# Attention and mixer on one core: q and k of batches 1 to 3 turned by DMA, scores in 64 rows, PSUM banks 4/2/2

## The chip, the cores and the metric

The kernel runs on one core of a Trainium2 chip. The metric is the device time of an execution in microseconds (us). A profiled execution also gives a trace; its span runs from the first to the last instruction. Engine names in profiles: PE is TensorE's matmul, PEld its weight load, DVE is VectorE, ACT is ScalarE, POOL is GpSimd, SP is SyncE; L376 is line 376 of the kernel that was profiled.

## The reference

Four batches of eight heads, 768 positions, head size 64. First a windowed attention with a distance bias, then a mixer with a low-rank product over the positions and a feed-forward of width 2048:

```python
scores = scale * np.matmul(q, k.transpose(0, 1, 3, 2))
rel = pos[:, None] - pos[None, :]
is_global = pos[None, :] < 8
is_local = (rel >= 0) & (rel < 96)
dist = np.where(is_global & ~is_local, 96.0, np.abs(rel))
scores = np.where(is_global | is_local, scores - slopes[:, None, None] * dist, -1e9)
a = softmax(scores)                      # over the last axis
x = np.matmul(a, v)                      # then heads side by side: (B, 768, 512)
h = x.transpose(0, 2, 1) @ U @ V         # U (768, 32), V (32, 768)
u = x + h.transpose(0, 2, 1)
out = u + np.maximum(u @ w_ch1, 0.0) @ w_ch2
```

## The kernel before

A *pair* is two heads of one batch, so there are 16 pairs, four to a batch; pair i belongs to batch i // 4. The 768 positions are six blocks of 128. Because the window is shorter than a block, a block of keys meets only its own block of queries and the next, where the eight global keys ride in eight places of the neighbour block (kA, vA).

For each pair these steps run:

- `load_qk`: two DMAs on SP's queue bring q and k of two heads as fp32 (tiles qst, kst, three buffers each; runs of 1536 bytes, position p * 6 + n in partition p). `cast_qk` makes fp16 (q16, k16, two buffers), on POOL except at the very start. `load_v`: two DMAs on POOL's queue, one per head, which convert to fp16 on the way, in runs of 64 elements (four buffers).
- `st_T`: six PE transposes each for q and k, into two PSUM tiles `tp`; ScalarE and VectorE copy them out as z[0], z[1] (tile qz, one per head, with zeros in the other head's 64 rows) and kT; kA is copied from kT with the global keys put in.
- Scores (`scores`): per head eleven 128x128 matmuls that contract over 128 rows, of which the other head's 64 are zero in qz; three chunks c of at most 512 columns, each in one PSUM tile `sc`. Batch 0 (`st_SE`) adds the bias by one more matmul and takes the exponential out of PSUM. Batches 1 to 3 (`st_S`) add the bias on VectorE with a scalar_tensor_tensor into sp (fp32, one buffer per head), and `st_E` takes the exponential of a whole head on ScalarE (tile ep).
- `st_V`: eleven matmuls per head into `ob`, normalised by VectorE into x_sb, then copied by POOL to fp16 as x16.
- `st_M1` and `st_M2`: the low-rank product (PSUM tiles tmp_ps and ups), written as uT by VectorE and ScalarE.

When a batch's attention is done, `queue_ff` puts its feed-forward into the deque `units`: per half batch 16 up units (`mk_up`: four matmuls into PSUM tile hps, then a Relu on ScalarE into htr) and twelve down units (`mk_down`: a quarter of a 128-row output tile each, in PSUM tile cps). `fill(n)` emits n of them between the attention steps of the next batch, 14 per pair. Batch 3's feed-forward runs alone at the end.

PSUM has eight banks, divided by tag: `sc` has three, `oc` two (ob and cps), `th` three (tp, tmp_ps, ups, hps).

Batch 0 is emitted under `manual_schedule`, that is, in the written order. After `ordered.close()` the tile framework's scheduler decides the order of each engine's queue; every queue then executes in order, so an instruction that waits holds up all that stand behind it on its engine. DMAs issued by POOL stand in POOL's queue among its copies and also wait for the eighth DMA before them on that queue.

Of the kernel before, what the change touches and what calls it, by code (L numbers as in the profile page):

```python
# [11 lines left out]
FP32 = mybir.dt.float32  # L12
FP16 = mybir.dt.float16
# [3 lines left out]
ALU = mybir.AluOpType  # L17
# [3 lines left out]
def kernel(  # L21
# [13 lines left out]
    nc = tc.nc  # L35
    B, H, S, D = q.shape
    NG = int(n_global)
    NL = int(n_local)
    P = 128
    DM = H * D  # L40
    NSB = S // P
# [4 lines left out]
    NP = H // 2  # L46
    qk_scale = 1.0 / math.sqrt(D)
# [5 lines left out]
    slope = [2.0 ** (-8.0 * (h + 1) / H) for h in range(H)]  # L53
# [5 lines left out]
    W = 256 * NSB - P  # L59
# [5 lines left out]
    stp = ctx.enter_context(tc.tile_pool(name="stp", bufs=2))  # L65
    kp = ctx.enter_context(tc.tile_pool(name="kp", bufs=2))
    scp = ctx.enter_context(tc.tile_pool(name="scp", bufs=2))
# [3 lines left out]
    psum = ctx.enter_context(tc.tile_pool(name="psum", bufs=1, space=bass.MemoryType.PSUM))  # L71

    def ps_sc():
        return psum.tile([P, 512], FP32, name="sc", tag="sc", bufs=3)

    def ps_oc(name):
        return psum.tile([P, 512], FP32, name=name, tag="oc", bufs=2)

    def ps_th(name, dtype=FP32, cols=512):
        return psum.tile([P, cols], dtype, name=name, tag="th", bufs=3)  # L80


    NVB = 4
# [2 lines left out]
    def load_qk(i):  # L86
        b, h0 = i // NP, 2 * (i % NP)
        got = []
        for src, nm in ((q, "qst"), (k, "kst")):
            st = stp.tile([P, 2, NSB, D], FP32, name=nm, tag=nm, bufs=3)  # L90
            nc.sync.dma_start(
                st.rearrange("p h n d -> p h (n d)"),
                src[b, h0:h0 + 2].rearrange("h (p n) d -> p h (n d)", n=NSB),
            )
            got.append(st)
        staged[i] = got

    def cast_qk(i, eng):
        got = []
        for st, nm in zip(staged.pop(i), ("q16", "k16")):  # L100
            st16 = stp.tile([P, NSB, 2, D], FP16, name=nm, tag=nm, bufs=2)
            eng.tensor_copy(st16.rearrange("p n h d -> p h n d"), st)  # L102
            got.append(st16)
        cast[i] = got

    def load_v(i):
        b, h0 = i // NP, 2 * (i % NP)
        vt = vbuf[i % NVB]
        for hi in range(2):
            nc.gpsimd.dma_start(  # L110
                vt[:, hi, :, 0:D], v[b, h0 + hi].rearrange("(n p) d -> p n d", p=P)
            )
        vts[i] = vt

    NPAIR = B * NP
    staged, cast, vts = {}, {}, {}


    ordered = ExitStack()
# [9 lines left out]
    def warm(n):  # L129
# [12 lines left out]
        out=relB, in_=relB, compare_op=ALU.is_ge, fill=BIG,  # L142
# [3 lines left out]
        out=relB, in_=relB, compare_op=ALU.is_ge, fill=BIG,  # L146
# [13 lines left out]
    def slopes(h0, h1):  # L160
        for h in range(h0, h1):
            nc.vector.tensor_scalar_mul(slI[:, h], ident16, slope[h] / qk_scale)
# [8 lines left out]
    relcat = cst.tile([P, 3, 256], FP32, name="relcat")  # L171
# [39 lines left out]
    kts, kas, vas = {}, {}, {}  # L211

    def st_T(i):
        stq, stk = cast.pop(i)
        kT = kp.tile([P, S], FP16, name="kT", tag="kT")
        kA = kp.tile([P, NSB - 1, P], FP16, name="kA", tag="kA")
        tps = []
        for st in (stq, stk):

            tp = ps_th("tp", FP16, S)  # L220
            tps.append(tp.rearrange("d (n p) -> d p n", n=NSB))
            for n in range(NSB):
                nc.tensor.matmul(  # L223
                    tp[:, n * P:(n + 1) * P], st[:, n].rearrange("s h d -> s (h d)"), ident16,
                    is_transpose=True, start=(n == 0), stop=(n == NSB - 1),
                )
        tq, tk = tps
        z = qz[i % 2]
        nc.scalar.copy(z[0][0:D].rearrange("d (p n) -> d p n", n=NSB), tq[0:D])
        nc.vector.tensor_copy(kT.rearrange("d (p n) -> d p n", n=NSB), tk)  # L230
        nc.vector.tensor_copy(kA.rearrange("d n p -> d (n p)"), kT[:, 0:S - P])  # L231
        nc.vector.tensor_copy(
            kA[:, 1:, 0:NG], kT[:, 0:NG].unsqueeze(1).broadcast_to((P, NSB - 2, NG))
        )
        nc.vector.tensor_copy(z[1][D:P].rearrange("d (p n) -> d p n", n=NSB), tq[D:P])  # L235
        kts[i], kas[i] = kT, kA

    def st_A(i):
        vt = vts[i]
        vA = vap.tile([P, 2, NSB - 1, D + 1], FP16, name="vA", tag="vA")  # L240
        nc.gpsimd.tensor_copy(vA, vt[:, :, 0:NSB - 1])  # L241
        nc.vector.tensor_copy(
            vA[0:NG, :, 1:],
            vt[0:NG, :, 0:1].broadcast_to((NG, 2, NSB - 2, D + 1)),
        )
        vas[i] = vA

    sps, eps = {}, {}

    def scores(i, hi, c, on_pe):  # L250
        h = 2 * (i % NP) + hi
        kT, kA, z = kts[i], kas[i], qz[i % 2][hi]
        sc = ps_sc()
        c0 = 512 * c
        tot = min(512, W - c0)
        r0 = 256 if c else 0
        if on_pe:
            nc.tensor.matmul(
                sc[:, 0:tot], slI[:, h], rel16.rearrange("p a c -> p (a c)")[:, r0:r0 + tot], start=True, stop=False
            )  # L260
        for kb in (2 * c, 2 * c + 1):
            o = 256 * kb - c0
            nc.tensor.matmul(  # L263
                sc[:, o:o + P], kT[:, kb * P:(kb + 1) * P], z[:, kb * P:(kb + 1) * P],
                start=(o == 0 and not on_pe), stop=(o + P == tot),
            )
            if kb < NSB - 1:
                nc.tensor.matmul(  # L268
                    sc[:, o + P:o + 2 * P], kA[:, kb], z[:, (kb + 1) * P:(kb + 2) * P],
                    start=False, stop=(o + 2 * P == tot),  # L270
                )
        return sc, c0, tot, r0

    def st_SE(i, c):

        if c == 0:
            for hi in range(2):
                eps[i, hi] = scp.tile([P, W], FP16, name=f"ep{hi}", tag=f"ep{hi}")
        for hi in range(2):
            sc, c0, tot, _ = scores(i, hi, c, True)  # L280
            nc.scalar.activation(  # L281
                eps[i, hi][:, c0:c0 + tot], sc[:, 0:tot], AF.Exp, scale=qk_scale
            )

    def st_S(i, c):
        if c == 0:
            sps[i] = [
                scp.tile([P, W], FP32, name=f"sp{hi}", tag=f"sp{hi}", bufs=1)
                for hi in range(2)
            ]  # L290
        relf = relcat.rearrange("p a c -> p (a c)")
        for hi in range(2):
            sc, c0, tot, r0 = scores(i, hi, c, False)
            nc.vector.scalar_tensor_tensor(  # L294
                out=sps[i][hi][:, c0:c0 + tot], in0=sc[:, 0:tot],
                scalar=qk_scale / slope[2 * (i % NP) + hi], in1=relf[:, r0:r0 + tot],
                op0=ALU.mult, op1=ALU.add,
            )
# [129 lines left out]
    for i in range(NP):  # L428
        st_SE(i, 0)
        if i == 0:  # L430
            cast_qk(2, nc.gpsimd)
        if i >= 2:
            st_M1(i - 2)
        else:
            warm(1)
        if i:
            st_V(i - 1, 0)
            st_V(i - 1, 1)
        if i == 0:
            load_v(3)  # L440
        if i:
            cast_qk(i + 2, nc.gpsimd)
        st_SE(i, 1)
        st_T(i + 1)
        if i < 3:
            slopes(2 * i + 2, 2 * i + 4)
        if i:
            load_qk(i + 3)
        if i >= 2:
            st_M2(i - 2)  # L450
        if i == 1:
            for c in range(4):
                load_w1(c)
        st_SE(i, 2)
        st_A(i)
        if i >= 2:
            load_v(i + 2)
        if i == 2:
            table(relcat)
        if i == 3:  # L460
            for c in range(4):
                load_w2(c)
# [10 lines left out]
    new_batch(1)  # L473
    for i in range(NP, NPAIR):
        b, hp = divmod(i, NP)
        if i + 3 < NPAIR:
            load_qk(i + 3)
        if i + 2 < NPAIR:
            load_v(i + 2)
        st_A(i)  # L480
        for c in range(3):
            st_S(i, c)
            fill(1)
        st_E(i, 0)
        st_E(i, 1)
        if i > NP:
            st_M2(i - 1)
            if hp == 0:
                queue_ff(b - 1, 0)
                queue_ff(b - 1, 1)  # L490
        fill(2)
        if i + 1 < NPAIR:
            if hp == NP - 1:
                new_batch(b + 1)
            st_T(i + 1)
        if i + 2 < NPAIR:
            cast_qk(i + 2, nc.gpsimd)
        fill(3)
        st_V(i, 0)
        fill(2)  # L500
        st_V(i, 1)
        fill(3)
        st_M1(i)
        fill(1)
# [39 lines left out]
```

## Time and profile before

| | |
|---|---|
| runs of the kernel (us) | 281.81, 284.34, 282.52; median 282.52 |
| span of the profiled execution | 279.8 us (its own device time is not listed; the runs lie 2.0 to 4.5 above this span) |
| PE busy | 255.3 us, 91% |
| PEld busy | 156.1 us, 56% |
| DVE, ACT, POOL busy | 147.8, 123.2, 87.2 us |
| mean granted TensorE clock | 0.963 |
| DMA packets | 42327, 26.64 MB; 26912 under 512 bytes |

Busy times overlap and matmuls are pipelined: a 128x128 matmul counts 0.22 us from its start to its end, while the next one may start 0.055 us after it. In what follows the start-to-start time is used for TensorE's work. In the group lines the columns are: line, engine, operation, output<-input by tile names, shape, count, busy us and mean ns of one, and the idle time of that engine just before the group with what ended it. In the lines in order of time the columns are start, duration (to the end of the last one where several are merged), engine, line, operation; in square brackets stands the idle time before. In the table of DMA issues the last column is the median time from issue to landing in us.

### The profile page before, as it was taken

How to read it: one execution, taken by the hardware profiler on the slowest of the kernel's cores; microseconds unless marked ns; L12 is line 12 of the kernel's file. 1: busy time of each engine (PE TensorE's matmuls, PEld its weight loads, DVE VectorE, ACT ScalarE, POOL GpSimd, SP SyncE). 2: the span in 40 equal slices, each digit the busy share in tenths (PEclk: the TensorE clock that was granted, in tenths of full speed). 3: DMA queues.
4: the chain of work that ended last, by engine and by line, in shares of the span. 5: the costliest groups of instructions: out<-in, count | busy, mean ns of one | idle time of the engine just before them, and what ended most of it. 6: DMA issues, size and time to landing. Idle time of an engine off the chain costs nothing.

```text
span 279.8 us, 5080 instructions
## 1 busy us (share of the span) xinstructions
PE 255.3 (91%) x2076; PEld 156.1 (56%) x2076; DVE 147.8 (53%) x301; ACT 123.2 (44%) x209; POOL 87.2 (31%) x129
## 2 busy tenths in 40 slices
PE   7765775899998999799999999999999999999994
PEld 3544554566556655566456655675566555545541
DVE  6766799156666564755957575754574440010011
ACT  2434551565218650668037630856076604604700
POOL 8948688360425124330606042300200010000000
PEclk9779896699999999999999999999999999999999
DMA  6999999992462527170634023000110021001001
GB/s 220 277 281 181 198 233 235 227 239 25 150 105 15 128 63 152 55 127 2 164 79 40 2 43 64 37 2 0 75 41 0 2 76 40 0 37 75 2 37 75
DMA packets 42327, 26.64 MB, mean 95 GB/s; under 512 B 26912, under 2 KB 39232, under 8 KB 42304
## 3 DMA queue, kind: packets, MB, share of 16 engines
q0 software_dynamic: 30144, 7.44, 27.5%
q1 hardware_dynamic: 12160, 18.88, 20.0%
q8 instruction: 16, 0.26, 0.4%
q14 instruction: 7, 0.06, 0.1%
HBM read 27.46 MB, written 6.29 MB: 121 GB/s over the span
## 4 chain that ended last, share of the span: by engine, by line
PE 62%; DVE 8%; ACT 4%; issue 2%; ACTq 0%
PE hps L376 25%; PE cps L395 24%; ACT ep L302 3%; PE tp L223 3%; DVE sp L294 2%; PE sc L268 2%; PE cps L389 2%; PE sc L263 2%; DVE qz L235 2%; DVE kT L230 2%; DVE osb L401 1%; PE tmp_ps L336 1%; PE ob L318 1%; PE ups L352 1%; PE ups L347 1%
## 5 line engine op out<-in xcount | busy, mean ns | idle before, releaser
L376 PE MATMUL hps<-uT,w 128*128 128x384 f16 x512 | 93.4, 328 | 1.3 <-DVE uT L358 1.3
L395 PE MATMUL cps<-w,htr 128*128 128x512 f16 x384 | 91.3, 379 | 0.0
L380 ACT ACTIVATE htr<-hps 128x384 f16<-128x384 f32 x128 | 61.8, 491 | 55.8 <-PE hps L376 55.1
L376 PEld LDWEIGHTS <-w 128*128 128x128 f16 x512 | 48.9, 98 | 30.7 <-issue 3.8
L395 PEld LDWEIGHTS <-htr 128*128 128x128 f16 x384 | 36.1, 98 | 37.4 <-issue 0.4
L302 ACT ACTIVATE ep<-sp 128x1408 f16<-128x1408 f32 x24 | 31.7, 1368 | 39.5 <-DVE sp L294 39.5
L294 DVE SCALAR_TENSOR_TENSOR sp<-sc,relcat 128x512 f32<-128x512 f32 (+1 forms) x72 | 41.8, 637 | 8.6 <-PE sc L268 8.3
L401 DVE TENSOR_TENSOR osb<-cps,x_sb 128x512 f32<-128x512 f32 x24 | 16.6, 690 | 49.6 <-PE cps L395 49.4
L110 POOL DMA_DIRECT2D v<-in_v_dram x32 | 27.3, 857 | 26.1 <-PE ob L318 13.9
L328 POOL CAST x<-x_sb 128x384 f16<-128x384 f32 x32 | 16.4, 514 | 52.5 <-DVE x_sb L325 52.3
L263 PE MATMUL sc<-qz,kT 128*128 128x128 f16 x192 | 30.4, 228 | 1.7 <-DVE qz L235 1.3
L230 DVE COPY kT<-tp 128x768 f16<-128x768 f16 x16 | 15.3, 957 | 28.0 <-PE tp L223 28.0
L268 PE MATMUL sc<-qz,kA 128*128 128x128 f16 x160 | 27.6, 230 | 1.9 <-DVE kA L231 1.3
L102 POOL CAST q<-qst 128x768 f16<-128x768 f32 x14 | 11.6, 830 | 56.8 <-issue 51.5
L268 PEld LDWEIGHTS <-kA 128*128 128x128 f16 x160 | 16.5, 103 | 10.5 <-issue 2.8
L318 PE MATMUL ob<-v,ep 128*128 128x65 f16 x192 | 17.9, 200 | 4.6 <-ACT ep L302 4.4
L263 PEld LDWEIGHTS <-kT 128*128 128x128 f16 x192 | 19.2, 103 | 4.6 <-DVE qz L235 0.9
L318 PEld LDWEIGHTS <-ep 128*128 128x128 f16 x192 | 14.6, 102 | 9.0 <-ACT ep L302 5.4
L281 ACT ACTIVATE ep<-sc 128x512 f16<-128x512 f32 (+1 forms) x24 | 12.6, 562 | 15.3 <-PE sc L268 15.1
L360 ACT CAST uT<-ups 128x384 f16<-128x384 f32 x16 | 7.5, 469 | 26.8 <-PE ups L352 26.8
L325 DVE TENSOR_TENSOR x_sb<-ob,rcp 128x384 f32<-128x384 f32 x32 | 17.7, 553 | 0.6
L314 PE MATMUL ob<-vA,ep 128*128 128x65 f16 x160 | 15.5, 200 | 0.9 <-POOL vA L241 0.5
(60 smaller groups left out, 236.9 us busy)
## 6 DMA issues: line engine op xcount, KB each, us to landing
qst<-in_q_dram SPq DMA_DIRECT2D x16, 384.0 KB, 5.7
kst<-in_k_dram SPq DMA_DIRECT2D x16, 384.0 KB, 6.1
out_dram<-osb SPq DMA_DIRECT2D x24, 256.0 KB, 2.0
w<-in_moe_w_ch_dram POOLq DMA_DIRECT2D x8, 512.0 KB, 11.9
v<-in_v_dram POOLq DMA_DIRECT2D x32, 96.0 KB, 6.2
u<-in_moe_U_dram POOLq DMA_DIRECT2D x1, 48.0 KB, 12.8
v16w<-in_moe_V_dram POOLq DMA_DIRECT2D x1, 48.0 KB, 11.4
```

The lines of the kernel that those rows point to most:

```text
L110: nc.gpsimd.dma_start(vt[:, hi, :, 0:D], v[b, h0 + hi].rearrange("(n p) d -> p n d", p=P))
L230: nc.vector.tensor_copy(kT.rearrange("d (p n) -> d p n", n=NSB), tk)
L263: nc.tensor.matmul(sc[:, o:o + P], kT[:, kb * P:(kb + 1) * P], z[:, kb * P:(kb + 1) * P], start=(o == 0 and not on_pe), stop=(o + P == tot),)
L268: nc.tensor.matmul(sc[:, o + P:o + 2 * P], kA[:, kb], z[:, (kb + 1) * P:(kb + 2) * P], start=False, stop=(o + 2 * P == tot),)
L294: nc.vector.scalar_tensor_tensor(out=sps[i][hi][:, c0:c0 + tot], in0=sc[:, 0:tot], scalar=qk_scale / slope[2 * (i % NP) + hi], in1=relf[:, ...
L302: nc.scalar.activation(ep, sps[i][hi], AF.Exp, scale=slope[2 * (i % NP) + hi])
L318: nc.tensor.matmul(ob[:, qi], ep[:, DG[qi]:DG[qi] + P], vt[:, hi, qi], start=(qi == 0), stop=True,)
L325: nc.vector.tensor_tensor(xo, ob[:, :, 0:D], rcp.unsqueeze(2).broadcast_to((P, NSB, D)), ALU.mult)
L376: nc.tensor.matmul(hps[:, 0:GT], w1_16[:, dc, jt * P:(jt + 1) * P], uT[:, dc, ts], start=(dc == 0), stop=(dc == NDC - 1),)
L380: nc.scalar.activation(cell["htr"][:, jt], hps[:, 0:GT], AF.Relu)
L395: nc.tensor.matmul(cps, htr[:, jc, t * P:(t + 1) * P], w2_16[:, jc], start=False, stop=(jc == NJC - 1),)
L401: nc.vector.tensor_tensor(osb, cps, x_sb[:, n], ALU.add)
```

## The change

Batches 1 to 3 (pairs 4 to 15) get q and k in another way, and PSUM banks are divided anew.

- `load_tok(i)` replaces `load_qk` and `cast_qk` for these pairs: four DMAs on POOL's queue, one per tensor and head, which convert to fp16 and put position n * 128 + p in partition p (runs of 64 elements, as v). The tiles qtm and ktm use the two buffers of q16 and k16.
- `turn(i)` replaces the PE transposes: two DMA transposes on SP's queue, 128x768 fp16 each, into qTd and kTd (kTd in the two buffers of kT).
- `st_G(i)` makes kA from kTd on VectorE, as `st_T` did from kT.
- `st_S2` replaces `st_S`: the two heads' scores are written alternately, each contracting over its own 64 rows, head 0 in rows 0 to 63 and head 1 in rows 64 to 127, into two `sc` tiles. The qz tiles are not used here.
- `sc` has four banks, `th` two, `oc` two as before.

Loads are emitted two pairs ahead and transposes one pair ahead. Batch 0 keeps its loads and PE transposes; the loads of pairs 4 and 5 and the transposes of pair 4 are emitted in batch 0's written order.

```diff
-        return psum.tile([P, 512], FP32, name="sc", tag="sc", bufs=3)
+        return psum.tile([P, 512], FP32, name="sc", tag="sc", bufs=4)
...
-        return psum.tile([P, cols], dtype, name=name, tag="th", bufs=3)
+        return psum.tile([P, cols], dtype, name=name, tag="th", bufs=2)
...
+    def load_tok(i):
+        b, h0 = i // NP, 2 * (i % NP)
+        got = []
+        for src, nm in ((q, "qtm"), (k, "ktm")):
+            st = stp.tile([P, NSB, 2, D], FP16, name=nm, tag=nm[0] + "16", bufs=2)
+            for hi in range(2):
+                nc.gpsimd.dma_start(
+                    st[:, :, hi], src[b, h0 + hi].rearrange("(n p) d -> p n d", p=P)
+                )
+            got.append(st)
+        tokmaj[i] = got
+
+    def turn(i):
+        got = []
+        for st, nm in zip(tokmaj.pop(i), ("qTd", "kTd")):
+            t = kp.tile([P, NSB, P], FP16, name=nm, tag={"kTd": "kT"}.get(nm, nm), bufs=2)
+            nc.sync.dma_start_transpose(t, st.rearrange("p n h d -> p (n h d)"))
+            got.append(t.rearrange("p n r -> p (n r)"))
+        headT[i] = got
+
+    def st_G(i):
+        qT, kT = headT[i]
+        kA = kp.tile([P, NSB - 1, P], FP16, name="kA", tag="kA")
+        nc.vector.tensor_copy(kA.rearrange("d n p -> d (n p)"), kT[:, 0:S - P])
+        nc.vector.tensor_copy(
+            kA[:, 1:, 0:NG], kT[:, 0:NG].unsqueeze(1).broadcast_to((P, NSB - 2, NG))
+        )
+        kas[i] = kA
...
+    def st_S2(i, c):
...
+        scs = [ps_sc(), ps_sc()]
+        half = [slice(0, D), slice(D, P)]
+        for kb in (2 * c, 2 * c + 1):
+            o = 256 * kb - c0
+            for hi in range(2):
+                nc.tensor.matmul(
+                    scs[hi][:, o:o + P], kT[half[hi], kb * P:(kb + 1) * P],
+                    qT[half[hi], kb * P:(kb + 1) * P],
+                    start=(o == 0), stop=(o + P == tot),
+                )
+            if kb < NSB - 1:
+                for hi in range(2):
+                    nc.tensor.matmul(
+                        scs[hi][:, o + P:o + 2 * P], kA[half[hi], kb],
+                        qT[half[hi], (kb + 1) * P:(kb + 2) * P],
+                        start=False, stop=(o + 2 * P == tot),
+                    )
+        for hi in range(2):
+            nc.vector.scalar_tensor_tensor(
...
-        if i:
+        if 0 < i < 2:
             cast_qk(i + 2, nc.gpsimd)
         st_SE(i, 1)
-        st_T(i + 1)
+        if i + 1 < NP:
+            st_T(i + 1)
...
-        if i:
-            load_qk(i + 3)
+        if i >= 2:
+            load_tok(i + 2)
+        if i == 3:
+            turn(NP)
...
-        if i + 3 < NPAIR:
-            load_qk(i + 3)
         if i + 2 < NPAIR:
+            load_tok(i + 2)
             load_v(i + 2)
+        if i + 1 < NPAIR:
+            turn(i + 1)
+        st_G(i)
         st_A(i)
...
-            st_T(i + 1)
-        if i + 2 < NPAIR:
-            cast_qk(i + 2, nc.gpsimd)
```

## The prediction

> **What bounds the kernel now.** I read the page's group table first, then busy time by stretches, then TensorE's and ScalarE's order of time, then the landing of the DMAs. Every number below is of the one profiled execution, whose span is 279.8 us; the median of the runs, 282.52, lies 2.7 above it, and I add 2.7 at the end.
>
> Groups (operation, shape, count, busy us and mean ns, idle time before it):
>
> ```profile
> L376 PE MATMUL hps<-uT,w 128*128 128x384 f16 x512 | 93.4, 328 | 1.3 <-DVE uT L358 1.3
> L380 ACT ACTIVATE htr<-hps 128x384 f16<-128x384 f32 x128 | 61.8, 491 | 55.8 <-PE hps L376 55.1
> L395 PE MATMUL cps<-w,htr 128*128 128x512 f16 x384 | 91.3, 379 | 0.0
> L263 PE MATMUL sc<-qz,kT 128*128 128x128 f16 x192 | 30.4, 228 | 1.7 <-DVE qz L235 1.3
> L302 ACT ACTIVATE ep<-sp 128x1408 f16<-128x1408 f32 x24 | 31.7, 1368 | 39.5 <-DVE sp L294 39.5
> L223 PEld LDWEIGHTS <-q 128*128 128x128 f16 x96 | 7.2, 106 | 3.5 <-DVE q L102 1.2 <-issue 1.2
> ```
>
> TensorE hardly idles before its large groups, while ScalarE and VectorE wait for it. Stretches (us, busy us of PE, PEld, DVE, ACT, POOL, then granted clock, DMA share, GB/s):
>
> ```profile
> 45.00:50.00 5.00, 1.98 (x18) 1.55 (x17) 3.41 (x8) 2.25 (x3) 4.11 (x7) 0.50 1.37 205
> 50.00:55.00 5.00, 4.73 (x27) 2.85 (x25) 1.30 (x4) 2.08 (x4) 1.74 (x3) 0.56 1.17 225
> 154.90:169.90 15.00, 14.79 (x129) 8.93 (x128) 9.61 (x19) 6.29 (x10) 4.94 (x7) 1.00 0.16 26
> 169.90:184.90 15.00, 14.90 (x130) 9.37 (x128) 8.80 (x18) 8.37 (x14) 3.23 (x5) 1.00 0.19 42
> ```
>
> So there are two regimes: up to about 52 us the kernel waits for data and small engines, with DMA full; after that a pair of heads takes 15 us and TensorE is the bound. TensorE's order of time shows the step between them, and the last two lines below show how ScalarE follows the dense feed-forward:
>
> ```profile
> 46.37 0.31 PE L263 MATMUL sc<-qz,kT 128*128 128x128 f16 x1
> 49.66 0.23 PE L318 MATMUL ob<-v,ep 128*128 128x65 f16 x1 [2.98 <-ACT ep L302]
> 52.17 4.50 PE L376 MATMUL hps<-uT,w 128*128 128x384 f16 x20
> 232.82 10.56 PE L376 MATMUL hps<-uT,w 128*128 128x384 f16 x64
> 234.97 0.49 ACT L380 ACTIVATE htr<-hps 128x384 f16<-128x384 f32 x1 [0.16 <-PE hps L376]
> 235.62 0.49 ACT L380 ACTIVATE htr<-hps 128x384 f16<-128x384 f32 x1 [0.16 <-PE hps L376]
> ```
>
> The first feed-forward matmul starts at 52.17 and the last one ends at about 275.8: 223.6 us. Its work by start-to-start times: 128 hps tiles at 0.65 (10.4 us for 16 tiles) are 83.2; 24 cps tiles at 0.22 + 16 x 0.216 are 88.1; eleven sets of tp at 0.75 are 8.2; eleven pairs of scores, 22 matmuls at 0.0555, are 13.4; ob 7.9, tmp_ps 4.0, ups 7.9. Sum 212.7, so about 11 us of this stretch is waiting.
>
> **The change, part by part.**
>
> *Transposes off TensorE.* Eleven sets of twelve leave the stretch: -8.2. With them go the kT and qz copies (958 and 961 ns on VectorE, 788 on ScalarE) and two POOL casts (0.83 each) per pair; their engines are not the bound, so I count only the waits of TensorE on kT, kA and qz, about 2 of the 11: -2.
>
> *Scores in 64 rows.* Pair 5's scores now stand ahead of the first hps in TensorE's order, so ten pairs remain: -1.2. If the two heads' matmuls run side by side, ten pairs cost 6.1 instead of 12.2; if not, they cost the same. No row shows two matmuls side by side, so the bounds are 0 and -6.1; I take half, -3.0, since some heads stand in runs of three or four without their partner, and since weight loads still come 22 to a pair.
>
> *Changing between 64 and 128 rows.* The compiled order has 41 groups of 64-row matmuls after the first hps, some of a single pair, hence 82 changes. No row shows one. Lower bound 0: the next load is hidden as now. Upper bound: a 128x128 matmul lasts 0.22 and the next starts 0.055 after it, so letting it run out costs 0.17, and an uncovered LDWEIGHTS 0.10: 0.27 each, 22 in all. I take the exposed load alone, 0.10: +8.2. The Trainium skill speaks against the change here: TensorEngine Tiling (Array Packing), Key Properties, says that changing the tiling mode, not merely the tile, drains TensorE. Taken at its word with the row's 0.17, this would be +14 rather than +8.2; no matmul in this trace has 64 rows, so the trace cannot confirm it.
>
> *PSUM 4/2/2.* With three th banks the dense stretch runs at 0.65 a tile. A tile's activation starts 0.85 after the tile's first matmul (234.97 against 232.82 + 2 x 0.65 = 234.12) and takes 0.49, and TensorE resumes some 0.06 after ScalarE (an ep ends at 175.83, ob starts at 175.89). A bank thus comes back after 1.40, while two tiles take 1.30: 0.05 a tile lost. Bounds: the 32 tiles of the tail alone, 1.6, and all 128, 6.4; with about 100 in dense runs, +5. The fourth sc bank saves nothing visible, since scores wait for sp and the exponentials.
>
> *Loads and transposes by DMA.* POOL issues four more loads per pair (0.82 each as for v, +3.3, less 1.7 of casts). POOL was busy 4.9 of 15 us, so that is hidden in steady state; without this cover each us would delay the x16 cast and so tmp_ps. SP gets two DMA transposes per pair, ahead of or behind outputs, which wait for osb; it issues little else. On the rings, back-to-back v loads land 0.75 apart (42.1 and 42.9), so six loads are 4.5 us per pair, two outputs 1.4 (three take 6.9% of 30 us), which leaves 9 of 15: the transposes are hidden if each holds the rings for under 4.5 us.
>
> It is not hidden at the seam between batch 0 and batch 1. Landing there:
>
> ```profile
> qst<-in_q_dram SPq DMA_DIRECT2D x16, 384.0 KB, 5.7
> kst<-in_k_dram SPq DMA_DIRECT2D x16, 384.0 KB, 6.1
> w<-in_moe_w_ch_dram POOLq DMA_DIRECT2D x8, 512.0 KB, 11.9
> v<-in_v_dram POOLq DMA_DIRECT2D x32, 96.0 KB, 6.2
> ```
>
> Pair 4 now needs four loads on POOL's queue behind the four w1 loads (issued from 22.9, landed 31.2 to 41.2); v loads issued at 31.9 and 32.7 landed at 42.1 and 42.9. I put pair 4's loads at 42.5, then two transposes. Their bounds: a quiet qst load lands in 3.0, one kst load under traffic took 9.4; for the two, 3 to 18.8. I take 4.5, the quiet pair of loads (3.0 to 3.5, issued 0.5 apart) with some traffic. So kT of pair 4 is there at 47 (today's kA: 41.4). Then kA copies 0.9, first scores 0.3, six sp steps 3.8, two exponentials 2.7: 54.7. In the compiled order TensorE has *all* scores of pair 5 ahead of tmp_ps and ups of pair 3 and the first hps; pair 5's sp reuses the buffers that the exponentials free at 54.7. Two sp steps, the last scores, tmp_ps, its cast, ups, uT's copy: 3.8 more. First hps at 58.5 instead of 52.17: +6.3. Bounds with the transposes': +2 and +32.
>
> The page VectorE: DVE Perf Modes of the skill, The three transpose paths, gives 1309 ns for one 128x128 block by DMA. Six blocks would be 7.9 us per transpose by that estimate, the two pairs would come at 58 and 74, and the start would move by some 25 us. No row here has a DMA transpose.
>
> A second wait follows. On VectorE the kA copies of pairs 6 and 7 stand ahead of the x_sb of pair 4's second head. Their loads queue behind w2 on POOL, whose last two issues wait for pair 5's landing (about 48) and which needs some 12 us more (it took 16.5 to the last landing): 61, then eight loads at 0.75, 67, transposes 71, kA 72, x_sb and x16 73.5. TensorE reaches tmp_ps of pair 4 after thirteen tiles, at 69: +4.5; bounds 0 and 10.
>
> Sum: -8.2 - 2 - 1.2 - 3.0 + 8.2 + 5 + 6.3 + 4.5 = +9.6. Span 289.4, with 2.7 around it 292.
>
> **Rivals.** *Faster (chance 0.22).* The halves overlap fully (-6.1), changing rows costs nothing, and the seam's DMAs come early (+2, no second wait): -8.2 - 2 - 1.2 - 6.1 + 5 + 2 = -10.5, about 272. For it: TensorE is the bound at 14.8 of 15 us, and it truly loses work. Against: two single-score groups per pair stand between 128-row matmuls. With the seam as I put it (+10.8) and full overlap, a change of rows must cost under 0.02 us for a gain at all; with the early seam, under 0.13.
>
> *No change (0.13).* Overlap and a cheap change of rows (0.04 each, +3.3) pay for the start: -17.5 + 5 + 3.3 + 6.3 + 4.5 = +1.6, about 284.
>
> *Much slower (0.20): transposes set the pace.* Each takes about the loaded 9.4 us, one after the other: pair 4 at 61, pair 5 at 80, first hps near 84, +32. In steady state 2 x 9.4 against 15 us per pair adds perhaps 3.8 for each of some eight pairs until the remaining feed-forward covers it less: 315 or more. For it: nothing in the trace shows a transpose; against: 192 KB is half of one qst load.
>
> *The forecast (0.45):* 278 to 302 by itself, from the bounds of the change of rows. That the change does not do what it says I rule out: the order shows 24 transposes on SP and no tp for pairs 4 to 15.
>
> **How the numbers follow.** A measurement of this kernel tells about 1% (2.8 us) from no change. Faster 0.22 and same 0.13 are those rivals; slower 0.65 is the forecast and the slow transposes. The likeliest is 292; the range reaches down nearly to the fast rival, 275, and up past the forecast's own end, 310, which leaves out the tail of the slow transposes.
>
> **What would show it.** Right: first hps near 58; dense tiles 0.70 apart; gaps of 0.1 at the first matmul after a change of rows; a VectorE wait for a DMA near 70. Wrong: transposes landing in under 3 us with the first hps by 54; 64-row matmuls starting in couples, with no gap around them; or a pair period that follows the DMA queue instead of TensorE.

## The result and the profile after

The changed kernel took 295.84 us (median of 295.68, 295.99, 296.87 and 294.36), the kernel before 282.59 beside it: a ratio of 1.0468, with a 95% interval from 1.0418 to 1.0517. The span of its profiled execution is 293.9 us, 14.1 longer than before.

The split by the first feed-forward matmul, which the prediction used, tells where the 14.1 lie. First, TensorE's order of time in the stretch that leads to it:

```profile
44.26 0.80 PE L404 MATMUL tmp_ps<-x,u 128*128 128x128 f16 x6 [5.33 <-POOL x L396]
62.72 0.39 PE L349 MATMUL sc<-qTd,kTd 64*128 64x128 f16 x4 [11.34 <-DMA kTd<-ktm]
67.49 0.50 PE L415 MATMUL ups<-v16w,tmp 128*128 128x384 f16 x1 [1.10 <-DVE tmp L408]
68.96 1.44 PE L444 MATMUL hps<-uT,w 128*128 128x384 f16 x4
```

The first hps starts at 68.96 instead of 52.17: 16.8 us are lost. From there to the end it is 224.9 us (293.9 - 69.0), before 227.6 (279.8 - 52.2): 2.7 are gained. So 16.8 - 2.7 = 14.1, and the loss lies in the start alone. The granted TensorE clock is no rival: by stretches of 5 us it is 0.50 from 45 to 70 us here and 0.50 to 0.56 from 45 to 55 before, so both kernels reach their first hps at about half clock, and from 75 us on it is 1.00 in both. One wait makes up most of the loss: for 11.34 us TensorE stands before pair 5's first score, because kTd of that pair has not landed. The view of the tile kTd says how unusual that is (its last line, from issue to landing):

```profile
DMA to landing us min/median/max: 2.5/2.7/11.9
```

The groups and DMA issues that answer to those shown before:

```profile
L444 PE MATMUL hps<-uT,w 128*128 128x384 f16 x512 | 94.4, 327 | 0.7 <-ACT htr L448 0.2
L349 PE MATMUL sc<-qTd,kTd 64*128 64x128 f16 x144 | 16.8, 234 | 12.3 <-DMA kTd<-ktm 11.3
L142 DVE COPY kA<-kTd 128x640 f16<-128x640 f16 x12 | 4.8, 404 | 36.7 <-DMA kTd<-ktm 36.7
L125 POOL DMA_DIRECT2D qtm<-in_q_dram x24 | 19.8, 835 | 39.1 <-DMA qTd<-qtm 34.6
...
w<-in_moe_w_ch_dram POOLq DMA_DIRECT2D x8, 512.0 KB, 10.2
...
qTd<-qtm SPq DMA_TRANSPOSE x12, 2.8
```

Two queues now stand still for transposes: VectorE, 36.7 us before its kA copies, and POOL, 34.6 us before it may load q into a buffer that a transpose still reads. Both also hold the work on x (x_sb on VectorE, x16 on POOL), which TensorE needs next; the 5.33 us before tmp_ps in the first fence are of that kind.

### The profile page after: what moved, and what is told of

It reads as the page before. It is cut to its first block, busy times and chain, and to the rows that moved or that the text cites. A ratio compares the mean times of both kernels' runs of the same rounds, so it can differ in the third digit from the quotient of the medians.

```text
span 293.9 us, 4802 instructions
## 1 busy us (share of the span) xinstructions
PE 251.5 (86%) x1930; PEld 139.7 (48%) x1932; DVE 125.5 (43%) x277; ACT 115.1 (39%) x197; POOL 108.0 (37%) x153
## 3 DMA queue, kind: packets, MB, share of 16 engines
q0 software_dynamic: 67776, 12.16, 52.8%
q1 hardware_dynamic: 24832, 14.16, 18.4%
## 4 chain that ended last, share of the span: by engine, by line
PE 60%; DMA 17%; POOL 9%; DVE 6%; issue 5%; ACT 2%; SPq 1%; POOLq 0%; ACTq 0%; DVEq 0%
PE cps L463 26%; PE hps L444 22%; DMA kTd<-ktm 7%; DMA v<-in_v_dram 6%; DVE sp L362 3%; DMA qtm<-in_q_dram 3%; POOL qtm L125 2%; PE cps L457 2%; POOL ktm L125 2%; DMA qTd<-qtm 2%; PE ups L415 2%; PE ob L386 2%; PE tmp_ps L404 1%; PE sc L349 1%; ACT ep L370 1%
## 5 line engine op out<-in xcount | busy, mean ns | idle before, releaser
L444 PE MATMUL hps<-uT,w 128*128 128x384 f16 x512 | 94.4, 327 | 0.7 <-ACT htr L448 0.2
L463 PE MATMUL cps<-w,htr 128*128 128x512 f16 x384 | 93.1, 380 | 0.0
L125 POOL DMA_DIRECT2D qtm<-in_q_dram x24 | 19.8, 835 | 39.1 <-DMA qTd<-qtm 34.6
L349 PE MATMUL sc<-qTd,kTd 64*128 64x128 f16 x144 | 16.8, 234 | 12.3 <-DMA kTd<-ktm 11.3
L125 POOL DMA_DIRECT2D ktm<-in_k_dram x24 | 20.0, 850 | 1.7 <-DMA w<-in_moe_w_ch_dram 1.7
L142 DVE COPY kA<-kTd 128x640 f16<-128x640 f16 x12 | 4.8, 404 | 36.7 <-DMA kTd<-ktm 36.7
L386 PE MATMUL ob<-v,ep 128*128 128x65 f16 x192 | 19.6, 205 | 0.9 <-ACT ep L370 0.9
L386 PEld LDWEIGHTS <-ep 128*128 128x128 f16 x192 | 15.6, 105 | 6.7 <-issue 2.4
L311 ACT ACTIVATE ep<-sc 128x512 f16<-128x512 f32 (+1 forms) x24 | 12.5, 562 | 14.1 <-PE sc L298 13.8
L349 PEld LDWEIGHTS <-kTd 64*128 64x128 f16 x144 | 8.2, 99 | 20.0 <-DMA kTd<-ktm 11.6
L391 DVE RECIPROCAL rcp<-ob 128x6 f32<-128x6 f32 x32 | 6.1, 190 | 26.8 <-PE ob L386 26.8
## 6 DMA issues: line engine op xcount, KB each, us to landing
w<-in_moe_w_ch_dram POOLq DMA_DIRECT2D x8, 512.0 KB, 10.2
```

The costliest lines, as they stand in the source:

```text
L125: nc.gpsimd.dma_start(st[:, :, hi], src[b, h0 + hi].rearrange("(n p) d -> p n d", p=P))
L349: nc.tensor.matmul(scs[hi][:, o:o + P], kT[half[hi], kb * P:(kb + 1) * P], qT[half[hi], kb * P:(kb + 1) * P], start=(o == 0), stop=(o + P ...
L386: nc.tensor.matmul(ob[:, qi], ep[:, DG[qi]:DG[qi] + P], vt[:, hi, qi], start=(qi == 0), stop=True,)
L444: nc.tensor.matmul(hps[:, 0:GT], w1_16[:, dc, jt * P:(jt + 1) * P], uT[:, dc, ts], start=(dc == 0), stop=(dc == NDC - 1),)
L463: nc.tensor.matmul(cps, htr[:, jc, t * P:(t + 1) * P], w2_16[:, jc], start=False, stop=(jc == NJC - 1),)
```

## What happens at the start

Pair 5's kTd is issued at 50.82, in the middle of the four w2 loads (issued from 49.72). The DMA view of 57.0 to 61.5 us, by queue (packets, MB, their time as a share of 16 engines), shows what the engines do meanwhile; q0 carries POOL's loads, here w2, and q1 the transposes of SP:

```profile
DMA packets 1268, 0.80 MB, mean 177 GB/s; under 512 B 644, under 2 KB 1268, under 8 KB 1268
...
q0 software_dynamic: 641, 0.64, 84.7%
q1 hardware_dynamic: 627, 0.16, 29.9%
```

641 packets of w2 against 627 of transposes: one for one. A packet of w2 has 1024 bytes and takes 0.10 us (the mean over the eight loads of w), a transpose packet 256 bytes and 0.02 us. A transpose of 128x768 is 768 such packets, 48 on each of 16 engines; if each waits for one packet of w2, that is 48 x 0.12 = 5.8 us, by estimate. In the trace, kTd's packets go out from 55.3 to 62.1, 6.8 us; in a quiet stretch the whole landing takes 2.5. The other 4.5 us lie between the issue and the first packet. qTd's data packets end at 52.1, w2's begin at 52.3, and for the next 3 us the engines work almost only for w2. The same pair's qTd, issued at 48.78, counts as landed only at 55.28, and kTd's first packet goes out 0.07 us later. So kTd may stand behind qTd's completion; but in other pairs kTd's packets begin up to 1 us ahead of it, so what holds the transpose back stays open.

The Trainium skill has the rule, in DMA: Bandwidth & Descriptors, Queues, rings and completion order: an engine goes round the queues that have work for it, a packet at a time. This trace agrees (641 packets to 627), and the prediction had not used it.

How much of the 16.8 us is this landing? By an estimate from these times: had kTd landed 2.5 us after its issue, at 53.3, and the rest had followed as it did (6.2 us from pair 5's first score to the first hps), the first hps would come at 59.6. So 9.4 us are the slow landing, and 7.4 the later issue of pair 5's transposes and what follows them.

## The experiments

The first theory was that the loss sits in the late start, and the start in pair 5's transposes beside w2. Its rivals: the new division of PSUM banks, the changes between 64 and 128 rows, and later the new loads. Ratios are to the kernel before on the same chip, with 95% intervals.

**The banks alone.**

```
-  tag="sc", bufs=3 ... tag="th", bufs=3
+  tag="sc", bufs=4 ... tag="th", bufs=2      # in the kernel before
```

> The kernel before with nothing changed but the PSUM banks (four for scores, two for sums and transposes, two for the dense products, instead of three, two, three). Theory (the loss is the late start of the first feed-forward product, made by pair 5's transposes): the banks cost 0.04 to 0.05 us for each of the 128 dense tiles, so +4 to +7 us, and the first feed-forward product stays within 1 us of 52.2. Rival (the banks are most of the loss): +10 us or more. A fourth bank for scores that pays for the lost dense bank would give 0 to +2.

Measured: 301.61 us, ratio 1.0682 [1.0624, 1.0739], +19.7. The first product stays at 52.7. TensorE's waits (total us, times, longest) name a large part of the cause:

```profile
PE hps L376 <- DVE kT L230: 6.3, 5, 2.7
PE ups L347 <- DVE qz L235: 3.7, 2, 2.2
```

Dense tiles and low-rank tiles wait until VectorE has copied a transposed k or q out of a th bank. With PE transposes in the kernel, two th banks are too few. The two lines make up 10.0 of the 19.7 us; the rest was not followed up. The result refutes my +4 to +7 for this kernel, but says nothing yet on the changed one, where tp is nearly gone.

**The changed kernel with the old banks.**

```
-  tag="sc", bufs=4 ... tag="th", bufs=2
+  tag="sc", bufs=3 ... tag="th", bufs=3      # in the changed kernel
```

> The changed kernel with the banks set back to 3/2/3. Theory: the late start stays (first feed-forward product near 69), the dense tiles go back to 0.65 us, so 4 to 6 us less than the changed kernel, about 290 to 292 us, still slower than before. Rival (the banks are the loss): 283 or less. If four score banks are what lets the couples overlap, no gain: 295.

Measured: 296.06 us, ratio 1.0486 [1.0412, 1.0561], no gain over the changed kernel. The first product is at 68.2. After it, neighbouring hps matmuls start 0.1677 us apart on the mean instead of 0.1712, which is 1.8 us over 512 of them; without the gaps of 0.3 us and more, which are waits or half clock, it is 0.1632 instead of 0.1692, or 3.1 us. So the dense tiles do get faster, but tmp_ps waits 8.6 us for x16 in this stretch instead of 3.7, and the granted clock falls to 0.76 and 0.56 between 80 and 90 us, where the changed kernel has 1.00. The banks are not the loss, and the 4 to 6 us that I expected back do not show in the time.

**The scores' rows alone.**

```
+  for hi in range(2):     # st_S of the kernel before, two sc tiles, heads alternating
+      matmul(scs[hi][...], kT[half[hi], ...], z[hi][half[hi], ...])
```

> The kernel before, q and k still turned on TensorE and the banks 3/2/3, with only the scores of pairs 4 and later taken over 64 rows, two heads alternating on the two halves of the array. Theory: the couples overlap in full (about -6.1 us over 12 pairs) and some 82 changes of row mode at 0.10 us give back +8.2, so +2 us, between -1 and +5. Rival (row changes are the loss): +8 or more. Rival (the overlap is a clear gain, changes cost nothing): -4 or less.

Measured: 287.81 us, ratio 1.0183 [1.0123, 1.0244], +5.9, a little above my interval. There are 42 changes into 64 rows and 42 out of them after the first product, at a median of 0.096 and 0.097 us beyond the usual distance of two matmuls: 8.1 us. Neighbouring 64-row matmuls start 0.038 us apart on the mean (without the six gaps over 0.07), against 0.030 in the changed kernel and 0.0555 with 128 rows: the heads run side by side less fully here. Why was not tried.

**A change of rows by itself.**

```
+  if extra and dc in (1, 3):          # last batch's up tiles, kernel before
+      matmul(wps[:, 0:P], zw[0:extra, 0:P], zw[0:extra, 0:P])   # extra: 64, then 128
```

> The kernel before with one added 128x128 matmul on a tile of zeros after the second and the fourth matmul of each up tile of the last batch's feed-forward, written to a spare sc bank: in the first half batch (16 tiles, 32 added matmuls) it contracts over 64 rows, in the second over 128. It measures the change of row mode by itself. With 128 rows each added one costs its 0.055 us, 1.8 in all. If a change costs 0.096 us into 64 rows and 0.097 out of them, each 64-row one costs 0.25, 8.0 in all, so 16 up tiles take 18.4 us in the first half against 12.2 in the second. If the trace's gaps at the changes came from something else, both halves take the same.

Measured: 291.02 us, a single execution, read only for the distances inside it. TensorE's order of time, first with 64 rows, then with 128:

```profile
233.50 0.23 PE L382 MATMUL sc<-zw 64*128 64x128 f16 x1
233.66 0.50 PE L376 MATMUL hps<-uT,w 128*128 128x384 f16 x2
234.09 0.23 PE L382 MATMUL sc<-zw 64*128 64x128 f16 x1
...
262.11 0.22 PE L382 MATMUL sc<-zw 128*128 128x128 f16 x1
262.17 0.49 PE L376 MATMUL hps<-uT,w 128*128 128x384 f16 x2
262.49 0.22 PE L382 MATMUL sc<-zw 128*128 128x128 f16 x1
```

From one added matmul to the next it is 0.59 us with 64 rows and 0.38 with 128: 0.21 for two changes, 0.105 each. Over 32 added matmuls that is 18.9 against 12.2 us; 18.4 and 12.2 were expected.

**The changed kernel without 64-row matmuls.**

```
+  nc.vector.tensor_copy(z[0][0:D], qT[0:D])    # st_G; scores from z and kT over 128 rows
+  nc.vector.tensor_copy(z[1][D:P], qT[D:P])
```

> The changed kernel with its DMA transposes and banks 4/2/2, but with scores over 128 rows: VectorE copies the two halves of qTd into the zero-padded qz tiles, and no 64-row matmul is left. Theory A (a change of row mode costs 0.096 us into 64 rows and 0.097 out of them, 41 of each after the first feed-forward product, 7.9 us; running two heads side by side returns about 5.0): 3 us less than the changed kernel in the stretch after the first feed-forward product, the start still near 69, so about 293. Rival (the side-by-side run is worth more than the changes cost): 297 or more. Rival (row changes are most of the loss): 287 or less.

Measured: 296.15 us, ratio 1.0511 [1.0441, 1.0581], no difference from the changed kernel that this can resolve. The first product is at 69.4; from there it is 224.1 us, 0.8 less than in the changed kernel instead of 3. As far as this can tell, the changes of rows and the side-by-side run nearly cancel; the rows are not the loss.

**The first loads earlier.**

```
-  if i >= 2: load_tok(i + 2)
+  if i == 1: load_tok(NP); load_tok(NP + 1)    # own buffers, ahead of w1
```

To make room, the fp32 tiles qst and kst have two buffers each here instead of three.

> The changed kernel (banks 4/2/2) with buffers of their own for the fp16 q and k, and the loads of pairs 4 and 5 issued ahead of w1, so that their transposes run long before w2 comes in. Theory: the transposes of pair 5 land in under 6 us, TensorE no longer waits some 11 us for them, the first feed-forward product comes at 53 to 58 instead of 69, and the time is 280 to 286. Rival (the transposes or row changes of the steady part are the loss): the first product comes earlier but the time stays above 291.

Measured: 298.62 us, ratio 1.0563 [1.0492, 1.0635]: a miss. The first product came at 62.7 instead of 53 to 58, and TensorE then stopped again, for a kTd of pair 6:

```profile
62.74 2.52 PE L444 MATMUL hps<-uT,w 128*128 128x384 f16 x12
77.28 0.40 PE L349 MATMUL sc<-qTd,kTd 64*128 64x128 f16 x4 [11.53 <-DMA kTd<-ktm]
```

The wait moved one pair on: part of that pair's loads are issued behind w2 (from 53.11), and its kTd could be issued only at 72.6 or later. On POOL a load waited 7.53 us for a transpose to free its buffer, and the v loads stood behind it. The run did not take the transposes away from big loads, either: kTd now lands in 5.2 us at most, but the qTd of pair 5, issued at 31.89 among the w1 loads, took 10.2, and those of pairs 6 and 7, beside w2, 11.8 and 10.8. From 36 to 41 us, beside w1, 775 packets of POOL's loads stand against 754 of the transposes.

**w2 out of the way.**

```
-  if i == 3: ... load_w2(c)         # at the end of batch 0's written order
+  if i == NP + 1: ... load_w2(c)    # after ordered.close()
```

The scheduler puts these loads near the front of POOL's queue: they are issued from 1.4 to 13.2 us.

> The changed kernel with the four loads of w2 at the front of POOL's queue, so that they land before pair 5's transposes are issued. Theory A1 (pair 5's transposes land late because w2 is on the rings at that time): pair 5's kTd lands within 6 us of its issue instead of 11.9, first feed-forward product at 57 to 63 instead of 69, time 284 to 292. Rival A2 (the rings carry a fixed amount of work before the first product, whatever its order): the 2 MB of w2 only push v, w1 and pair 4 back, the first product stays at 66 or later, time 293 or more.

Measured: 293.56 us, ratio 1.0411 [1.0355, 1.0466]. The transposes do come sooner: pair 5's kTd lands in 5.6 us and the worst one, of pair 6, in 7.2; TensorE waits 4.37 for pair 5's instead of 11.34. But w2 now delays v and what follows (5.94 us before ob for vA, 6.35 before tmp_ps for x16), and the first product is at 70.3. So the landing followed A1, but the start and the time followed the rival A2: what is moved out of one wait shows up in another. Nor is 2.5 us reached away from w2, with the other loads of the start beside the transposes.

**Only pairs 8 and later**, two runs, with banks 3/2/3; the second with 128-row scores.

```
+  N0 = 8     # load_tok, turn and st_G for i >= N0; load_qk, cast_qk and st_T below
```

> The changed way of loading and turning, and the 64-row scores, from pair 8 on only; batches 0 and 1 as before; banks 3/2/3. It takes the transposes away from the crowded start. Theory A (the start is the loss): first feed-forward product at 52 to 53 as before, no wait of TensorE for a DMA above 2 us, and the steady part gains: eight sets of transposes at 0.75 are -6.0, waits on them -1, about 56 changes of row mode at 0.097 are +5.4, running side by side -3.4: 277 to 280. Rival (the transposes on SP and the loads on POOL hurt anywhere): 285 or more.

> As the run that changes pairs 8 and later only, but with scores over 128 rows from zero-padded qz tiles that VectorE fills from qTd; banks 3/2/3; no 64-row matmul. Theory A: -6.0 for the transposes and -1 for waits, nothing for row changes: 275 to 277, some 2 us below its 64-row sister. Rival (the side-by-side run pays for its changes): 1 us or more above the sister. Rival (VectorE's extra copies delay x_sb): 282 or more.

Measured: 285.81 us, ratio 1.0145 [1.0083, 1.0208], and 283.98 us, ratio 1.0062 [1.0022, 1.0101]. Without the transposes beside w2 the first product is at 54.5 and 51.2, and some 10 us of the loss are gone. 128 rows are 1.8 us better than 64, as expected, though the intervals touch. But no gain is left, against my -4 to -7. In the profiled execution of the second run (280.88 us, its fastest) TensorE's waits after the first product are these:

```profile
PE tmp_ps L406 <- POOL x L398: 7.6, 5, 3.9
PE ob L388 <- ACT ep L372: 0.9, 2, 0.7
```

Before, tmp_ps waited 0.2 us there for x16. POOL's order of time has the reason, q loads that stand until a transpose frees their buffer, with x16 behind them:

```profile
79.30 1.64 POOL L125 DMA_DIRECT2D qtm<-in_q_dram  x2 [3.59 <-DMA qTd<-qtm]
88.21 1.64 POOL L125 DMA_DIRECT2D qtm<-in_q_dram  x2 [5.27 <-DMA qTd<-qtm]
```

**Transposes and loads, each alone.** These two runs tell apart what the start's extra DMA is: the new loads (3072 packets of 128 bytes a pair instead of 512 of 1536) or the transposes.

```
+  nc.sync.dma_start_transpose(t, st...)   # turn_only: from q16, k16; then st_T's four copies
```

```
+  cast[i] = got    # end of load_tok, tok_pe: new loads, st_T's PE transposes kept
```

> One part of the change alone. Loads of q and k, casts, 128-row scores and banks 3/2/3 as before; only the PE transposes of pairs 4 and later become DMA transposes on SP (from q16 and k16), and the same four copies to qz, kT and kA read qTd and kTd instead of PSUM. Theory L (the late start comes from the loads: in the trace of the changed kernel a pair's q and k cost 3072 packets of 128 bytes at 33 ns, 6.3 us on all 16 rings, against 512 packets of 1536 bytes at 76 ns before, 2.4 us; its two transposes add 1536 packets of 256 bytes at 23 ns, 2.2 us): the start moves by 2 to 5 us, the stretch after it gains 8.2 for the transposes and 1 to 2 of waits, so 276 to 281. Rival T (the transposes themselves are late beside w2, as the 11.9 us landing suggests): first feed-forward product at 60 or later, 288 or more.

> The other part alone: q and k of pairs 4 and later come by the changed kernel's four converting loads on POOL's queue in runs of 64 elements, but are turned on TensorE as before; 128-row scores and banks 3/2/3. Theory L (3.9 us more of the 16 rings for each pair, on a crowded start): first feed-forward product at 57 to 66 instead of 52, the steady part about as before or 1 to 3 us worse, 287 to 296. Rival T (the transposes are the cause): first product within 2 us of before and 280 to 284.

In turn_only qTd and kTd have one buffer each.

Measured: transposes alone 295.22 us, ratio 1.0424 [1.0311, 1.0536]; loads alone 283.48, ratio 1.0062 [1.0024, 1.0100]. My favoured theory L fell. With the loads alone the first product is at 52.8; with the transposes alone it is at 63.0, and TensorE's longest waits are

```profile
PE sc L272 <- DVE kT L239: 9.1, 1, 9.1
...
PE tmp_ps L345 <- ACT htr L389: 7.8, 1, 7.8
```

The first is pair 5 again: its kTd, issued at 43.60, lands after 11.4 us. (The worst, 11.8, is pair 6's, issued at 58.61.) The second is ScalarE's Relu standing behind a qz copy that waited 7.41 us for qTd. The DMA view of this kernel from 49.0 to 53.5 us, the time of pair 5's transposes and of w2, repeats the pattern with other loads of q and k (pair 5's kTd has its packets from 49.1 to 54.5):

```profile
q0 software_dynamic: 687, 0.64, 87.5%
q1 hardware_dynamic: 681, 0.18, 34.1%
```

**Transposes alone, after w2.**

```
+  if 8 <= i + 1 < NPAIR: turn(i + 1)      # otherwise as turn_only
```

> As the run with DMA transposes alone (old loads, casts, copies, 128-row scores, banks 3/2/3), but only from pair 8 on, after w2 has landed. Theory W (a transpose's packets go out one for one with those of a big load on the same rings, so only the neighbourhood of w2 makes them late): landings of 2.5 to 5 us throughout, the first feed-forward product at 52 as before, no wait of TensorE above 2 us that before has not, eight sets of PE transposes at 0.75 gone: 275 to 279, faster than before. Rival Q (the transposes also come late in the steady part, because they stand on SP's queue behind outputs, and the casts and copies that wait for them hold up ScalarE, VectorE and POOL): 281 to 286, with waits of TensorE for ScalarE's Relu or POOL's x16 in the stretch after 100 us.

Measured: 279.06 us, ratio 0.9900 [0.9855, 0.9944]: this version is 1.0% faster than the kernel before, a small gain but clear of its interval. Away from the big loads the transposes land quickly, and the first product is at 53.0. The view of its tile kTd, then TensorE's waits after 52 us:

```profile
DMA to landing us min/median/max: 2.5/2.5/4.0
```

```profile
PE hps L385 <- ACT htr L389: 2.9, 4, 0.9
PE ob L327 <- ACT ep L311: 2.4, 4, 0.8
PE tmp_ps L345 <- POOL x L337: 1.3, 1, 1.3
PE ups L356 <- DVE tmp L349: 0.3, 1, 0.3
```

Eight sets of PE transposes at 0.75 are 6.0 us less. Of this 3.4 are given back as waits (6.9 here, 3.5 in the same stretch before), which leaves 2.6; the spans differ by 2.8. (From the first product on it is 224.1 us against 227.6, and the first product itself is 0.8 later.) Part of the return is plain: ScalarE's qz copy takes 1.54 us from qTd where it took 0.79 from PSUM, and Relu stands behind it.

## Why the prediction was right, step by step

The time (292 against 295.84) and the direction were right, as was the place of most of the loss, the seam between the batches. That the sum came so close was partly luck: the start was priced far too low, and four smaller terms too high.

- *The start, +6.3: measured +16.8.* This is the mis-sized term. I had pair 4's kT late (47; its kA copy starts at 42.85) and took pair 5 to wait only for sp buffers, free at 54.7. Its transposes, issued beside w2, landed at 62.7, and no term stood for them. The landing cost 9.4 us by the estimate above; the other 7.4 are close to the 6.3. The trace before had a row for it: a kst load issued at 49.42, among the same w2 loads, landed after 9.7 us. My price for a transpose, 4.5 us for two "with some traffic", was good in a quiet stretch only. The upper bound of +32, with one loaded kst landing of 9.4 us for each transpose, had nearly the right size for one of them (11.9). Runs: turn_only has the wait without the new loads, tok_pe does not have it, turn_from8 loses it.
- *Transposes off TensorE, -8.2.* Sound as work: eight of the eleven sets account for turn_from8's gain together with its new waits. That only other engines would feel it was wrong: VectorE, ScalarE and POOL stop for landings, and so hold x_sb, Relu and x16.
- *Running side by side, -3.0: about -5.7.* 64-row matmuls start 0.030 us apart on the mean, against 0.0555, over 220 matmuls: nearly the full bound of -6.1. TensorE's order of time shows couples, and a change of rows on either side:

```profile
186.76 1.04 PE L463 MATMUL cps<-w,htr 128*128 128x512 f16 x4
187.73 0.23 PE L349 MATMUL sc<-qTd,kTd 64*128 64x128 f16 x2
187.79 0.22 PE L356 MATMUL sc<-qTd,kA 64*128 64x128 f16 x2
187.85 0.22 PE L349 MATMUL sc<-qTd,kTd 64*128 64x128 f16 x2
188.00 0.39 PE L463 MATMUL cps<-w,htr 128*128 128x512 f16 x1
```

  The couples follow at 0.06. After four cps matmuls at 0.216 the next could start at 187.62 and starts at 187.73; after the last couple, at 187.91, and starts at 188.00.
- *Changes of rows, +8.2: 7.9.* 41 into 64 rows and 41 out, 0.096 and 0.098 us at the median; switch_tail has 0.105 by itself. (The median leaves out that 12 of the changes out took 0.17 to 0.38; they may hold other waits.) The exposed weight load was the row that fits: the load for the couple above starts only at 187.72, while before the change a load started 0.22 ahead of its matmul. (That the gap is the load's own time is not shown.) First the line after, then two of the kernel before:

```profile
187.72 0.10 PEld L349 LDWEIGHTS <-kTd 64*128 64x128 f16 x2 [0.42 <-issue]
...
172.02 0.10 PEld L263 LDWEIGHTS <-kT 128*128 128x128 f16 x1
172.24 0.22 PE L263 MATMUL sc<-qz,kT 128*128 128x128 f16 x1
```

  The Trainium skill, TensorEngine Tiling (Array Packing), Key Properties, has that a change of mode drains TensorE. That each change costs something agrees with it; a full drain is not shown, since the first 64-row matmul starts at 187.73, and the last cps before it ends at 187.80 by the trace's modelled ends. The full +14 by the row of 0.17 was too much.
- *Banks, +5: 1.4 to 3.2.* Neighbouring hps matmuls start 0.1712 us apart on the mean instead of 0.1685, 1.4 us over 512; without the gaps of 0.3 us and more (waits, half clock) it is 0.1692 instead of 0.1629, or 3.2. In one dense run the loss is near the 0.05 that I gave a tile:

```profile
245.88 11.24 PE L444 MATMUL hps<-uT,w 128*128 128x384 f16 x64
```

  The cps after it starts at 256.96, so 16 tiles take 11.08 us instead of 10.40, 0.04 more each. At 0.04 each, 3.2 us would be 80 tiles; I took about 100 at 0.05. after_323 confirms that the banks matter little for the time here.
- *The second wait, +4.5: 3.35*, before tmp_ps of pair 4 at 82.86. Its mechanism, x_sb behind kA copies that wait for a landing, was right: VectorE waits 4.67 us before the kA copy at 80.56, and the x_sb step behind it starts at 81.68.

The start erred by +10.5, the others by -2.7, -1.2, -0.3 and, for the banks, -3.6 to -1.8. Together that turns +9.6 into 12.3 to 14.1 of the measured 14.1. The terms -8.2, -2 and -1.2 stand in this as predicted; they were not measured apart, so the close sum proves little about them.

Of the rivals, the faster one needed an early seam and a change of rows under 0.13 us. It had the second, at 0.10, and a fuller overlap than I took; the late seam decided against it. "Transposes set the pace" was half right: they did so beside w2, not in steady state: from 100 us on they land in 2.5 to 3.9 us. The 7.9 us per transpose, estimated from the 1309 ns of the Trainium skill (VectorE: DVE Perf Modes, The three transpose paths), is too high in quiet and too low for pair 5.

## What to carry to other kernels

Price a DMA transpose by what shares the engines with it at that moment, not by its bytes: many small packets that alternate with the large ones of a weight load took over four times their quiet time (11.9 us against 2.5). So put it where no big load runs, or keep that part on TensorE; the version with DMA transposes from pair 8 on does both. Then ask which in-order queues will stand for its landing (loads that reuse its source, copies that read its output) and what else is queued on them. And when a resource such as a PSUM bank is divided anew, test the division with and without the rest of the change: here the same division cost 19.7 us in one kernel and next to nothing in the other.

## What the runs showed of the hardware

- A DMA transpose of 128x768 fp16 is issued in 1.21 us and lands in 2.5 at best, and in 11.9 beside a 2 MB weight load with which it alternates packet for packet (627 to 641 in 4.5 us), after a pause of 3 us that the runs don't explain. Beside the start's other loads, without the weights, pair 5's took 5.6.
- Two 64-row matmuls on different halves of the array run side by side in the changed kernel: a couple every 0.058 us, where one 128-row matmul takes 0.0555.
- A change between 64 and 128 rows costs 0.096 to 0.098 us each way at the median in the changed kernel, and 0.105 in a run made for it.
- A copy of 64x768 fp16 by ScalarE took 1.54 us from SBUF, read with a stride of 128 elements, and 0.79 us from a PSUM tile in the same pattern.
